# Fewer, wider VectorE operations in the convolution of a mixer kernel, and a GpSimd copy that orders its tokens

## Chip, cores, metric

The kernel runs on one core of one Trainium2 chip. The metric is the device time of one execution in microseconds: before the change 1099.98, the median of three runs (1099.77 to 1100.17). One further execution was profiled.

## What is computed

A block over 2048 tokens of 576 channels: a layer norm, then two branches on the normalised tokens, an S4D convolution over time and an MLP over channels, and a gate.

```python
x  = A_u
xn = layernorm(x)
# branch A: kernel K[d, l] = 2 Re sum_n C[d, n] exp(A[d, n] dt[d] l),  l < 2048, 128 modes n
s  = irfft(rfft(xn, 4096) * rfft(K, 4096))[:2048] + xn * D_skip
# branch B: per token, 576 -> 4608 -> 576
h  = gelu(layernorm(xn) @ w1 + b1)
out = x + s * silu(h @ w2 + b2)
```

## The kernel before, in words

**MLP.** The inner dimension is cut into 12 groups of 384 and the tokens into four blocks of 512, which gives 48 slots. A slot is three tiles of the first layer (`layer1`, L599: 14 matmuls of 512 columns each), GELU on ScalarE (L635), a split of the result into a high part (ScalarE, L638) and a low part (VectorE, L641), and the second layer (`layer2`, L662: 72 matmuls of 288 columns), whose sums VectorE adds to `acc` (L672). Numbers are split in this way so that three products of the faster fp32r format stand for one in fp32; weights are split on the fly (L552 on ScalarE, L549 on VectorE). A prologue `pair` (L582) can do two of the remainder matmuls at the edge of a slot as one step.

**Convolution.** Two parts, both on all five engines.

- *Kernel tables* (`tables`, `kgen`), 36 blocks of 16 channels. VectorE makes phases (L897, L900, L906), ScalarE rounds them and takes cosine and sine (L903 to L916), VectorE makes magnitudes (L922) and weighs the phases with them (`weigh`): 32 late columns go to a tile `U` (L933), 32 reversed early ones to one half of `v` (L935), 32 early ones to the other half (L937, and L939 with a minus sign). Each of these is done once for the cosine plane and once for the sine plane. Then PE multiplies `U` with `v` (L978) and ScalarE copies the block out (L983). The phase tile `w` has two buffers.
- *Transforms* (`chunk`), six chunks of 96 channels. Tokens `xc` and kernel `kt` are split (`in_parts`: high L1058 on ScalarE, low L1062 on VectorE; the tokens are read in another order than they lie in memory, so with a step), transformed (`x1` L1082, `k1` L1113), transposed by VectorE in 32x32 blocks from PSUM (L1090, L1121, two halves of a bank pair apiece), transformed again (`s2` L1143), multiplied: ScalarE copies the kernel's spectrum (L1152), VectorE makes four products per frequency in two operations (L1158) and adds and subtracts them (L1164, L1165). Then come the inverse transforms (L1185, L1211) and stores.

**Order.** The order of all instructions is planned in Python while the program is recorded. A class `Order` keeps a clock for each engine; each `step` has an engine, an assumed duration, the marks that it needs and one that it sets. MLP units are placed on PE one after the other. Between them `advance` places steps of VectorE, ScalarE and GpSimd whose needs are met by the assumed clocks, and `pe_turns` places the convolution's PE steps in the gaps between MLP units. A `kgen` can ride in front of `x1`, `k1`, `s2` or another host (`ride`, `lead`), without a gap of its own. Once recorded, each engine works through its instructions in that order and waits on semaphores; the assumed durations have no further effect. GpSimd also issues DMAs, in its one queue: parameters `par` (L879), stores of the convolution's result (L1220), the loads and stores of the last sums (L701 to L713).

Of the kernel before, what the change touches and what calls it, by code (L numbers as in the profile page):

```python
# [9 lines left out]
F32 = mybir.dt.float32  # L10
F32R = mybir.dt.float32r
# [7 lines left out]
P = 128  # L19
# [20 lines left out]
def dve(n):  # L40
    return 0.075 + 0.00104 * n


def act(n):
    return 0.06 + 0.00098 * n
# [165 lines left out]
def mixer_kernel(ctx, tc, u, log_a_real, a_imag, c_real, c_imag, log_dt, d_skip, w1, b1, w2, b2,  # L211
# [558 lines left out]
    def params():  # L770
# [8 lines left out]
        dt = sb.tile([P, 2, SB, 32], F32, name="U").rearrange("p a b c -> p (a b c)")[:, :D]  # L779
# [108 lines left out]
    def tables(b):  # L888
# [36 lines left out]
        def weigh(k, part):  # L925

            if k == 0 and part == 0:
                T["v"] = sb.tile([P, 2, SB, 64], F32, name="v")
                T["U"] = sb.tile([P, 2, SB, 32], F32, name="U")
                TAB[b] = (T["U"], T["v"])  # L930
            w, v, m = T["w"], T["v"], T["m"]
            if part == 0:
                nc.vector.tensor_mul(T["U"][:, k], w[:, k, :, 33:], m[:, :, 64:])  # L933
            elif part == 1:
                nc.vector.tensor_mul(v[:, k, :, :32], w[:, k, :, 32:0:-1], m[:, :, :32])  # L935
            elif k == 0:
                nc.vector.tensor_mul(v[:, k, :, 32:], w[:, k, :, :32], m[:, :, 32:64])  # L937
            else:
                nc.vector.scalar_tensor_tensor(v[:, k, :, 32:], w[:, k, :, :32], -1.0, m[:, :, 32:64],  # L939
                                               op0=OP.mult, op1=OP.mult)  # L940
# [5 lines left out]
                 step("DVE", dve(SB * NV), f(phase, 0), need=[("wu", b - 2, 1)] if b > 1 else []),  # L946
# [6 lines left out]
                + [step("DVE", dve(n), f(weigh, k, part), need=[("sin", b, k)] + ([("kg", b - 1)] if b else []),  # L953
                        mark=("wu", b, k) if part == 2 else None) for k in range(2) for part in range(3)])
# [10 lines left out]
    def kgen(b):  # L965
# [20 lines left out]
        return [step("PE", KG + 0.2, mm, need=need + [("wu", b, 1)], cv=1, mark=("kg", b)),  # L986
# [23 lines left out]
    def chunk(c):  # L1010
# [41 lines left out]
        def in_parts(which, i, get, m, need):  # L1052

            def high():
                a = sb.tile([P, 2, 4 * CH], F32R, name="pr").rearrange("p t c -> p (t c)")
                b = sb.tile([P, 2, 4 * CH], F32R, name="ys", bufs=2).rearrange("p t c -> p (t c)")
                PARTS2[which, i] = [t.rearrange("p (c b) -> p c b", b=m) for t in (a, b)]
                nc.scalar.activation(PARTS2[which, i][0], get(), AF.Copy)  # L1058

            def low():  # L1060
                a, b = PARTS2[which, i]
                nc.vector.tensor_sub(b, get(), a.bitcast(F32))  # L1062

            n = 768 if which == "k" else 2000
            four.append(step("ACT", act(n), high, need=need))
            four.append(step("DVE", dve(n), low, mark=(which + "p", c, i)))

        def x1(i):
# [18 lines left out]
            for d0 in (0, 24):  # L1087
                for e in range(2):
                    c0 = 48 * i + d0 + 12 * e
                    add("DVE", 0.65, lambda d0=d0, e=e, c0=c0: nc.vector.transpose(  # L1090
                        A2[:, :, 0, c0:c0 + 12].rearrange("p k d r -> p d k r"), Q[d0][:, e]), cv=-e)

        def k1(i):
# [7 lines left out]
            in_parts("k", i, lambda: KT[c, i], 64, [("k1", c, i - 1) if i else ("x1", c, CH // 48 - 1)])  # L1101
# [18 lines left out]
            for g in range(4):  # L1120
                add("DVE", 0.65, lambda g=g: nc.vector.transpose(  # L1121
                    A2[:, :, 1, 48 * i + 12 * g:48 * i + 12 * g + 12].rearrange("p k d r -> p d k r"),
                    Q[g // 2 * 2][:, g % 2]),
                    cv=-(g % 2))

        def s2(p):
# [5 lines left out]
            def mm():  # L1132
# [5 lines left out]
                for i in range(2):  # L1138
                    for ri in range(2):
                        for q in range(4):  # L1140
                            for f in range(2):
                                r = slice(64 * f, 64 * f + 64)
                                nc.tensor.matmul(Q[i][32 * q:32 * q + 32, f, 2 * ri:2 * ri + 2],  # L1143
# [6 lines left out]
            def copy(i):  # L1150
                KK[i] = sb.tile([P, 2, 2, CH], F32, name="kk")
                nc.scalar.activation(KK[i], Q[i][:, :, 1::2], AF.Copy)  # L1152

            def prod(i):

                PR[i] = sb.tile([P, 2, 4 * CH], F32, name="pr").rearrange("p t (a b d) -> p t a b d", a=2, b=2)
                for t in range(2):
                    nc.vector.tensor_mul(PR[i][:, t], bc(Q[i][:, t, 0::2], 2, 2), bc(KK[i][:, t], 1, 2))  # L1158

            def sums(i):  # L1160
                if i == 0:
                    Y.append(ys_tile())
                x, y = PR[i], Y[0]
                nc.vector.tensor_sub(y[:, i, 0], x[:, :, 0, 0], x[:, :, 1, 1])  # L1164
                nc.vector.tensor_add(y[:, i, 1], x[:, :, 0, 1], x[:, :, 1, 0])  # L1165
            for i in range(2):
                two.append(step("ACT", act(4 * CH), lambda i=i: copy(i), need=[("s2", c, p)]))
                two.append(step("DVE", 0.95, lambda i=i: prod(i), cv=-1))
                two.append(step("DVE", 0.63, lambda i=i: sums(i), mark=("sum", c, p) if i else None))
# [540 lines left out]
```

## Time and profile before

| | before |
|---|---|
| median of 3 runs | 1099.98 us |
| span of the profiled execution | 1099.5 us |
| VectorE busy | 920.5 us, 1514 instructions |
| ScalarE busy | 696.6 us, 1040 instructions |
| GpSimd busy | 184.6 us, 254 instructions |

The span runs from the first to the last profiled instruction. In the views, PE is TensorE, PEld its weight loads, DVE VectorE, ACT ScalarE, POOL GpSimd and SP the queue engine; a group's row names the line, engine, operation, output <- inputs, shape and count, then busy us, mean ns of one, and the idle time just ahead of them with what ended it. In a timeline, a row starts with start and length in us.

### The profile page before, as it was taken

The numbers are of one execution on the slowest core, as the hardware profiler recorded it, in microseconds if no ns is written. First come the engines' busy times: TensorE is split into PE (matmuls) and PEld (weight loads), VectorE is DVE, ScalarE is ACT, GpSimd is POOL, SyncE is SP. The second block draws the span as 40 slices with busy tenths as digits, with TensorE's granted clock in tenths as the row PEclk, the third lists the DMA queues.
The fourth block names the chain that finished last, engine by engine and source line by source line (L and its number), as shares of the span: only waits on it lengthen the run. The fifth ranks groups of instructions, "written<-read, shape, count | busy, mean of one in ns | idle before, by whom it ended". The sixth has DMA issues, their size and how long they took to land.

```text
span 1099.5 us, 27206 instructions
## 1 busy us (share of the span) xinstructions
PE 1090.1 (99%) x11447; PEld 953.9 (87%) x11447; DVE 920.5 (84%) x1514; ACT 696.6 (63%) x1040; POOL 184.6 (17%) x254
## 2 busy tenths in 40 slices
PE   9999999999999999999999999999999999999997
PEld 7989899889888888888998888888888888888896
DVE  7798678979998899999999998898998986765356
ACT  6585699866666675676865857566675754325233
POOL 5566211170110100001100000000100012110220
PEclk9999999999999999999999999999999999999999
DMA  8746655734444152455623314242333426453453
GB/s 230 235 144 156 232 162 196 215 75 126 154 124 145 48 112 57 116 121 143 150 57 94 91 56 126 39 147 60 90 92 77 143 65 180 117 177 108 126 149 94
DMA packets 139683, 138.23 MB, mean 126 GB/s; under 512 B 88952, under 2 KB 105016, under 8 KB 138984
## 3 DMA queue, kind: packets, MB, share of 16 engines
q1 hardware_dynamic: 124664, 85.49, 29.5%
q0 software_dynamic: 14336, 50.12, 14.8%
q8 instruction: 89, 1.46, 0.6%
q10 hardware_dynamic: 560, 0.89, 0.3%
q14 instruction: 34, 0.28, 0.1%
HBM read 102.17 MB, written 36.63 MB: 126 GB/s over the span
## 4 chain that ended last, share of the span: by engine, by line
PE 96%; SPq 1%; DMA 1%; DVE 1%; issue 0%; ACT 0%; ACTq 0%; DVEq 0%
PE mxb L662 21%; PE mxa L662 21%; PE mxa L599 20%; PE mxb L599 20%; PE cv L1143 3%; PE cv L978 3%; PE cv L1185 2%; PE cv L1211 2%; PE cv L1113 1%; PE cv L1082 1%; DMA w<-in_A_u_dram 1%; SPq L791 1%; PE mxa L614 0%; SPq L383 0%; DMA acc<-in_A_u_dram 0%
## 5 line engine op out<-in xcount | busy, mean ns | idle before, releaser
L641 DVE TENSOR_TENSOR hl<-h,hh 128x512 fp32r<-128x512 f32 x144 | 99.1, 691 | 88.3 <-ACT hh L638 87.6
L662 PE MATMUL mxb<-w2h,hh 128*128 128x288 f32 x576 | 171.6, 298 | 0.0
L662 PE MATMUL mxa<-w2h,hh 128*128 128x288 f32 x573 | 170.8, 298 | 0.0
L662 PE MATMUL mxb<-w2h,hl 128*128 128x288 f32 x576 | 170.1, 295 | 0.3 <-DVE hl L641 0.3
L662 PE MATMUL mxb<-w2l,hh 128*128 128x288 f32 x576 | 169.5, 294 | 0.0
L662 PE MATMUL mxa<-w2h,hl 128*128 128x288 f32 x573 | 169.1, 295 | 0.0
L662 PE MATMUL mxa<-w2l,hh 128*128 128x288 f32 x573 | 168.6, 294 | 0.0
L635 ACT ACTIVATE h<-mxa,b1t 128x512 f32<-128x512 f32 x73 | 50.2, 688 | 111.8 <-PE mxa L599 110.1
L662 PEld LDWEIGHTS mxa<-w2h,hh 128*128 128x128 f32 x573 | 107.6, 188 | 6.6 <-issue 3.5
L662 PEld LDWEIGHTS mxb<-w2h,hh 128*128 128x128 f32 x576 | 108.1, 188 | 5.7 <-issue 1.5
L662 PEld LDWEIGHTS mxb<-w2l,hh 128*128 128x128 f32 x576 | 108.1, 188 | 0.6
L662 PEld LDWEIGHTS mxb<-w2h,hl 128*128 128x128 f32 x576 | 108.1, 188 | 0.5 <-DVE hl L641 0.5
L662 PEld LDWEIGHTS mxa<-w2l,hh 128*128 128x128 f32 x573 | 107.6, 188 | 0.6
L662 PEld LDWEIGHTS mxa<-w2h,hl 128*128 128x128 f32 x573 | 107.5, 188 | 0.0
L879 POOL DMA_DIRECT2D par<-par_s x36 | 27.8, 773 | 464.2 <-DVE mg L922 459.5
L638 ACT ACTIVATE hh<-h 128x512 fp32r<-128x512 f32 x144 | 90.6, 630 | 3.6
L635 ACT ACTIVATE h<-mxb,b1t 128x512 f32<-128x512 f32 x71 | 48.9, 689 | 68.9 <-PE mxb L599 66.5
L672 DVE TENSOR_TENSOR acc<-mxa,acc 128x576 f32<-128x576 f32 x87 | 65.5, 752 | 31.4 <-PE mxa L662 31.0
L672 DVE TENSOR_TENSOR acc<-mxb,acc 128x576 f32<-128x576 f32 x88 | 66.1, 752 | 16.0 <-PE mxb L662 15.5
L599 PE MATMUL mxa<-XH,w1h 128*128 128x512 f32 x284 | 79.1, 400 | 0.0
L599 PE MATMUL mxb<-XH,w1h 128*128 128x512 f32 x280 | 77.8, 399 | 0.0
L599 PE MATMUL mxa<-XL,w1h 128*128 128x512 f32 x284 | 76.1, 390 | 0.0
(261 smaller groups left out, 2485.9 us busy)
## 6 DMA issues: line engine op xcount, KB each, us to landing
raw<-in_B_w_dram SPq DMA_DIRECT2D x72, 288.0 KB, 3.5
raw<-in_B_w_dram SPq DMA_DIRECT2D x96, 192.0 KB, 3.8
par_s<-A POOLq DMA_DIRECT2D x4, 2160.0 KB, 8.2
par<-par_s POOLq DMA_DIRECT2D x36, 240.0 KB, 3.6
f2t<-f2q SPq DMA_DIRECT2D x24, 256.0 KB, 3.3
g2t<-g2p SPq DMA_DIRECT2D x24, 256.0 KB, 4.0
bias<-XR SPq DMA_DIRECT2D x42, 128.0 KB, 3.8
raw<-in_B_w_dram SPq DMA_DIRECT2D x48, 96.0 KB, 4.0
```

Source lines behind the costliest of these rows:

```text
L599: nc.tensor.matmul(q, a, b, start=j == 0 and i not in BEGUN, stop=j == len(ops) - 1, skip_group_check=True)
L635: nc.scalar.activation(t, q, AF.Gelu_apprx_tanh, bias=b1t[:, k:k + 1], scale=1.0)
L638: LAST[0] = nc.scalar.activation(hh[:, i], t, AF.Copy)
L641: nc.vector.tensor_sub(hl[:, i], t, hh[:, i].bitcast(F32))
L662: nc.tensor.matmul(q[:, dh, :288], a[:, i, c], b[:, i, d], start=i == 0 and k == 0 and not alone, stop=i == G - 1 and k == 2)
L672: nc.vector.tensor_add(o, q[:, dh:dh + n, :288], b)
L791: nc.sync.dma_start(r[32 * g:32 * g + 32].rearrange("c (b n) -> c b n", n=32), dram(src[k], 32 * g, [[N, 32], [32 * N, D // 32], [1, 32]]))
L879: nc.gpsimd.dma_start(PAR[b].rearrange("p (g i) k -> p g (i k)", g=4), dram(par_s, (b // 3 * 48 + b % 3 * 4) * NPAR, [[D * NPAR, P], [12 * ...
L978: nc.tensor.matmul(q[32 * g:32 * g + 32, i // 2, i % 2 * 64:i % 2 * 64 + 64], U[:, ri, 4 * g + i, :], v[:, ri, 4 * g + i, :], start=ri == ...
L1143: nc.tensor.matmul(Q[i][32 * q:32 * q + 32, f, 2 * ri:2 * ri + 2], m[r, 4 * i + q, 32 * ri:32 * ri + 32], A2[r, 4 * p + 2 * i + q // 2, :, ...
L1185: nc.tensor.matmul(QI[q // 2][64 * f:64 * f + 64, q % 2, i], MAT["g2t", p + i // 2][r, i % 2, f, ri], YS[p + i // 2][0][r, i % 2, ri, f], ...
L1211: nc.tensor.matmul(Q[h][64 * y:64 * y + 64, t], g1t.rearrange("p a e -> p (a e)"), A2[:, k:k + 2, 1].rearrange("p i d r -> p i r d"), star ...
```

## The change

- **U over the phases.** The weighed late columns are written over the phase tile's own columns 33 to 64; tile `U` is gone. PE now reads its weights from `w`. The phases of block b so wait for `kgen` of block b-2 (`kg`), no longer for its weighing (`wu`).
- **Weighing.** Where both planes are weighed alike, one operation does both: four operations a block in place of six.
- **Tokens.** GpSimd copies them into the transform's order (`xt`); both split operations read this copy, without a step.
- **Transpositions.** One per bank pair in place of two.
- **Spectra.** `s2` writes the signal's and the kernel's two parts one after the other (`ri::2`), so each matmul's output is two runs of 96 elements in place of one of 192. ScalarE copies the kernel's spectrum with imaginary and real part in exchanged order, and adds a negated copy of the imaginary part. Overlapping views of this copy let one VectorE operation make all four products, and one addition all sums.
- The tile that the parameters' `dt` borrowed is another one, since `U` is gone. Assumed durations and marks of the planner follow.

```diff
-        def weigh(k, part):
-            if k == 0 and part == 0:
+        def weigh(part):
+            if part == 0:
                 T["v"] = sb.tile([P, 2, SB, 64], F32, name="v")
-                T["U"] = sb.tile([P, 2, SB, 32], F32, name="U")
-                TAB[b] = (T["U"], T["v"])
+                TAB[b] = (T["w"][:, :, :, 33:], T["v"])
             w, v, m = T["w"], T["v"], T["m"]
             if part == 0:
-                nc.vector.tensor_mul(T["U"][:, k], w[:, k, :, 33:], m[:, :, 64:])
+                nc.vector.tensor_mul(v[:, 0, :, 32:], w[:, 0, :, :32], m[:, :, 32:64])
             elif part == 1:
-                nc.vector.tensor_mul(v[:, k, :, :32], w[:, k, :, 32:0:-1], m[:, :, :32])
-            elif k == 0:
-                nc.vector.tensor_mul(v[:, k, :, 32:], w[:, k, :, :32], m[:, :, 32:64])
+                nc.vector.tensor_mul(v[:, :, :, :32], w[:, :, :, 32:0:-1], bc(m[:, :, :32], 1, 2))
+            elif part == 2:
+                nc.vector.tensor_mul(w[:, :, :, 33:], w[:, :, :, 33:], bc(m[:, :, 64:], 1, 2))
...
-                 step("DVE", dve(SB * NV), f(phase, 0), need=[("wu", b - 2, 1)] if b > 1 else []),
+                 step("DVE", dve(SB * NV), f(phase, 0), need=[("kg", b - 2)] if b > 1 else []),
...
+            def turn():
+                T["x"] = sb.tile([P, 24, m], F32, name="xt")
+                nc.gpsimd.tensor_copy(T["x"], get())
...
-                nc.scalar.activation(PARTS2[which, i][0], get(), AF.Copy)
+                nc.scalar.activation(T["a"], source(), AF.Copy)
...
-                nc.vector.tensor_sub(b, get(), a.bitcast(F32))
+                nc.vector.tensor_sub(T["b"], source(), T["a"].bitcast(F32))
...
+            if which == "x":
+                four.append(step("POOL", 2.3, turn, need=need))
+            four.append(step("ACT", act(768), high, need=need))
+            four.append(step("DVE", dve(768), low, mark=(which + "p", c, i)))
...
-                for e in range(2):
-                    c0 = 48 * i + d0 + 12 * e
-                    add("DVE", 0.65, lambda d0=d0, e=e, c0=c0: nc.vector.transpose(
-                        A2[:, :, 0, c0:c0 + 12].rearrange("p k d r -> p d k r"), Q[d0][:, e]), cv=-e)
+                c0 = 48 * i + d0
+                add("DVE", 0.9, lambda d0=d0, c0=c0: nc.vector.transpose(
+                    A2[:, :, 0, c0:c0 + 24].rearrange("p k d r -> p d k r"), Q[d0]), cv=-1)
...
-                                nc.tensor.matmul(Q[i][32 * q:32 * q + 32, f, 2 * ri:2 * ri + 2],
+                                nc.tensor.matmul(Q[i][32 * q:32 * q + 32, f, ri::2],
...
-                nc.scalar.activation(KK[i], Q[i][:, :, 1::2], AF.Copy)
+                nc.scalar.activation(KK[i][:, :, :2], Q[i][:, :, :1:-1], AF.Copy)
+                nc.scalar.activation(KK[i][:, :, 2], Q[i][:, :, 3], AF.Copy, scale=-1.0)
...
-                for t in range(2):
-                    nc.vector.tensor_mul(PR[i][:, t], bc(Q[i][:, t, 0::2], 2, 2), bc(KK[i][:, t], 1, 2))
+                nc.vector.tensor_mul(PR[i], bc(x, 2, 2), k)
...
-                nc.vector.tensor_sub(y[:, i, 0], x[:, :, 0, 0], x[:, :, 1, 1])
-                nc.vector.tensor_add(y[:, i, 1], x[:, :, 0, 1], x[:, :, 1, 0])
+                nc.vector.tensor_add(y[:, i].rearrange("p a t d -> p t a d"), x[:, :, :, :CH], x[:, :, :, CH:])
```

More of the change, by code (lines that the diff above doesn't have):

```diff
@@ L952, in tables @@
                  step("DVE", dve(n), f(mags, 1), mark=("mags", b))]
[L953 to L954 removed]
+                + [step("DVE", dve((1, 2, 2, 1)[part] * n), f(weigh, part), need=[("sin", b, part > 0)]
+                        + ([("kg", b - 1)] if b else []), mark=("wu", b) if part == 3 else None) for part in range(4)])
     KT = {}
```

41 lines of the change are left out of this document (20 added, 21 removed).

## The prediction

> **What bounds the kernel now.** I read the page first: engine shares, then the granted clock, then the chain that ended last.
>
> ```profile
> span 1099.5 us, 27206 instructions
> PE 1090.1 (99%) x11447; PEld 953.9 (87%) x11447; DVE 920.5 (84%) x1514; ACT 696.6 (63%) x1040; POOL 184.6 (17%) x254
> PEclk9999999999999999999999999999999999999999
> PE 96%; SPq 1%; DMA 1%; DVE 1%; issue 0%; ACT 0%; ACTq 0%; DVEq 0%
> ```
>
> PE is busy 1090.1 of 1099.5 us, at full clock in every slice, and 96% of the last chain is PE. VectorE is at 84%, but the chain holds 1% of it. A busy PE can still hide waits, since ends of matmuls are modelled, so the waits of PE come next (five rows in all; the two left out belong to the start-up), and one stretch of 200 us from the middle.
>
> ```profile
> PE mxa L1273 <- POOL XL L1266: 1.3, 1, 1.3
> PE cv L1143 <- issue: 0.6, 1, 0.6
> ...
> PE mxb L662 <- DVE hl L641: 0.3, 1, 0.3
> ```
>
> ```profile
> 600.00:800.00 200.00, 199.41 (x2632) 170.65 (x2631) 181.18 (x289) 133.73 (x177) 11.11 (x14) 1.00 0.31 84
> ```
>
> After the start PE waits twice in the whole execution, 0.6 us once (L1143, the second spectrum transform `s2`) and 0.3 us once (L662). The window's columns are length, then busy time of PE, PEld, DVE, ACT, POOL: PE misses 0.59 us of 200 while VectorE works 181. Nothing that VectorE, ScalarE or GpSimd does in this kernel is waited for by PE, except by luck of fractions of a microsecond. The end is the last matmul and a fixed tail:
>
> ```profile
> 1092.84 0.29 PE L662 MATMUL cv<-w2h,hl 128*128 128x288 f32 x1
> ```
>
> It ends at 1093.1, so 6.4 us of last gate, sum and store follow. The change touches none of them.
>
> So the time is the sum of PE's work plus two small waits, and the question for each edit is only: does it change PE's work, or make PE wait?
>
> **The change: PE's own work.** The instruction order of the two built programs shows the same 3456, 1946, 1152, 768, 768, 288, 144 and 48 matmuls of MLP layers and convolution steps, and 14 `pair` prologues in each. What differs is where the convolution's groups stand between the MLP's matmuls: PE leaves the MLP for a group 84 times before and 86 times after (without the start), and the kernel-table groups (`kgen`) that ride in front of another group go from 18 of 36 to 16. What a ride is worth can be read from three places of the timeline: `s2` alone, `kgen` with `s2`, `kgen` alone.
>
> ```profile
> 717.37 0.29 PE L662 MATMUL mxa<-w2h,hl 128*128 128x288 f32 x1
> 717.59 1.59 PE L1143 MATMUL cv<-A,f2t 64*32 64x192 f32 x64
> 719.11 0.40 PE L662 MATMUL mxb<-w2h,hh 128*128 128x288 f32 x1
> 719.34 0.30 PE L662 MATMUL mxb<-w2l,hh 128*128 128x288 f32 x1
> 719.48 0.29 PE L662 MATMUL mxb<-w2h,hl 128*128 128x288 f32 x1
> ```
>
> ```profile
> 744.29 0.29 PE L662 MATMUL mxa<-w2h,hl 128*128 128x288 f32 x1
> 744.51 1.10 PE L978 MATMUL cv<-v,U 128*32 128x64 f32 x64
> 745.54 1.61 PE L1143 MATMUL cv<-A,f2t 64*32 64x192 f32 x64
> 747.08 0.40 PE L662 MATMUL mxb<-w2h,hh 128*128 128x288 f32 x1
> ```
>
> ```profile
> 648.82 0.29 PE L662 MATMUL mxa<-w2h,hl 128*128 128x288 f32 x1
> 649.03 1.10 PE L978 MATMUL cv<-v,U 128*32 128x64 f32 x64
> 650.07 0.40 PE L662 MATMUL mxb<-w2h,hh 128*128 128x288 f32 x1
> ```
>
> An MLP matmul starts every 0.13 to 0.14 us (719.34 to 719.48). From the last one before a group to the first behind it: 1.74 us for `s2`, 2.79 for both, 1.25 for `kgen`. Less one normal step each that is 1.61, 2.66 and 1.12, and the second step after the return is 0.10 too long each time (719.11 to 719.34, against 0.13). A ride therefore saves 1.61 + 1.12 + 0.10 - 2.66 = 0.17 us. Two rides fewer: **+0.3 us**.
>
> The wait at L1143 stood here:
>
> ```profile
> 621.04 1.59 PE L1143 MATMUL cv<-A,f2t 64*32 64x192 f32 x61
> 623.22 0.53 PE L1143 MATMUL cv<-A,f2t 64*32 64x192 f32 x3 [0.59 <-issue]
> ```
>
> The last three of 64 records come late; against the normal 1.6 us the group loses 1.1 us. The trace names no releaser ("issue"), so it isn't VectorE's work that was late. The place is re-ordered by the change, so it may vanish (-1.1) or turn up elsewhere (0). I take the middle, **-0.5**. The 0.3 us at L662 lies ahead of the first transform, where both programs have the same PE order, and stays.
>
> Two PE instructions change form, and no row shows the new forms. `s2` writes each result as two runs of 96 instead of one of 192 (the spectra of signal and kernel are interleaved differently), and `kgen` takes its weights out of the phase table `w`, at a row step of 65 instead of 32. The floor for both is 0: same columns, same contraction, nothing that could shorten them. For the ceiling the trace offers only the groups' whole time: 24 groups of `s2` at 1.6 us are 39 us, 36 of `kgen` at 1.1 us are 40. A slowdown by a tenth would be 4 us for either. I take 0, because a matmul's rows here go by its columns (192 columns in 64 records at 1.6 us, 64 columns in 64 records at 1.1 us), and these don't change.
> The Trainium skill speaks against this edit: its page "PSUM — Partial Sum Buffer", section Specifications (TRN2), says that PSUM has 8-byte cachelines and that any non-contiguous access pattern slows matmuls significantly. No row of this trace has such an output; taken literally it is the third rival below, and with runs of 96 elements I read it as meaning short steps.
>
> **The change: the other engines.** These sums are off the path; they say how much room there is.
>
> ```profile
> L933 DVE TENSOR_TENSOR U<-w,mg 128x512 f32<-128x512 f32 x72 | 49.3, 684 | 3.7 <-PE cv L978 2.3 <-ACT w L914 0.7
> L922 DVE TENSOR_TENSOR mg<-par 128x1024 f32<-128x1024 f32 x36 | 44.0, 1223 | 0.7
> L1158 DVE TENSOR_TENSOR pr<-cv,kk 128x384 f32<-128x384 f32 x96 | 48.7, 550 | 2.0 <-ACT kk L1152 1.8
> L1121 DVE STREAM_TRANSPOSE A<-cv 128x384 f32<-128x384 f32 x48 | 24.5, 556 | 2.7 <-PE cv L1113 2.7
> L1164 DVE TENSOR_TENSOR ys<-pr 128x192 f32<-128x192 f32 x48 | 17.0, 355 | 1.0
> L1062 DVE TENSOR_TENSOR ys<-xc,pr 128x768 fp32r<-128x768 f32 x12 | 24.7, 2057 | 2.0 <-ACT pr L1058 2.0
> L1062 DVE TENSOR_TENSOR ys<-kt,pr 128x768 fp32r<-128x768 f32 x12 | 11.1, 928 | 0.0
> L1058 ACT ACTIVATE pr<-xc 128x768 fp32r<-128x768 f32 x12 | 25.2, 2103 | 13.1 <-DMA xc<-xn_s 12.8 <-DVE w L900 0.3
> L1058 ACT ACTIVATE pr<-kt 128x768 fp32r<-128x768 f32 x12 | 10.1, 838 | 3.8 <-PE cv L1082 3.3 <-ACT w2h L552 0.3 <-PE cv L1113 0.3
> L1152 ACT ACTIVATE kk<-cv 128x384 f32<-128x384 f32 x48 | 23.1, 482 | 24.7 <-PE cv L1143 13.8 <-DVE pr L1158 10.9
> L432 POOL TENSOR_SCALAR w<-w,mv,rs 128x576 f32<-128x576 f32 x6 | 16.5, 2755 | 17.4 <-ACT w2h L552 9.5 <-ACT h L635 7.8
> L549 POOL TENSOR_TENSOR w1l<-raw,w1h 128x384 fp32r<-128x384 f32 x2 | 2.0, 1018 | 0.1
> ```
>
> Weighing, 36 tables: six operations of 512 elements become two of 512 and two of 1024: 36 x (4 x 0.684 - 2 x 1.223) = 10.4 us less. Products: 96 x 0.55 become 48 of 768 elements at about 0.93 (the 768-element subtraction): 8 less. Sums: 96 x 0.355 become 48 of 384 at 0.55: 7.7 less. Transpositions: 96 x 0.556 become 48 at 0.93 to 1.11: 0 to 9 less. Low parts of the tokens: 12 x (2.06 - 0.93) = 13.5 less. VectorE gives up some **45 of 920 us**. ScalarE saves 12 x (2.10 - 0.84) = 15 on the tokens' high parts and adds 48 negated half-size copies, at most 48 x 0.48 = 23 and about half of that: even. GpSimd gains 12 copies of 768 elements. Its nearest rows put one between 2 x 1.02 = 2.0 us (L549, scaled) and 2.75 x 768 / 576 = 3.7 us (L432, scaled); if the strided read costs it the factor 2.10 / 0.84 that it costs ScalarE, 5.1. I take 2.8, between the two rows of its own.
>
> The path to the first transform `x1` was 2.10 + 2.06 = 4.2 us from loaded tokens to both parts; it becomes 2.8 + 0.84 + 0.93 = 4.6 (3.8 to 6.9). ScalarE's high part now waits for GpSimd, and behind it in ScalarE's queue stand GELUs of the next MLP tile, for which VectorE and then PE wait. The cover is shown by a place where that same step waited far longer:
>
> ```profile
> 940.63 2.11 ACT L1058 ACTIVATE pr<-xc 128x768 fp32r<-128x768 f32 x1 [9.94 <-DMA xc<-xn_s]
> 930.06 1.06 POOL L713 DMA_DIRECT2D out_dram<-row  x2 [10.17 <-DVE row L710]
> ```
>
> ScalarE stood 9.9 us for its tokens and the list of PE's waits has no entry for it. If that cover is missing, 12 transforms late by 0.4 us (at most 2.7) cost 5 us (at most 32).
>
> GpSimd's copy also runs beside VectorE. While GpSimd worked on 128x576 from 64.89 to 67.18, a VectorE subtraction took 0.92 us instead of its mean of 0.69 (this row and the mean are from the timeline and page):
>
> ```profile
> 64.89 2.29 POOL L432 TENSOR_SCALAR w<-w,mv,rs 128x576 f32<-128x576 f32 x1
> ```
>
> ```profile
> 65.34 0.92 DVE L641 TENSOR_TENSOR hl<-h,hh 128x512 fp32r<-128x512 f32 x1 [0.56 <-ACT hh L638]
> ```
>
> ```profile
> L641 DVE TENSOR_TENSOR hl<-h,hh 128x512 fp32r<-128x512 f32 x144 | 99.1, 691 | 88.3 <-ACT hh L638 87.6
> ```
>
> Some three VectorE operations beside each copy, 0.23 us each, are 12 x 0.7 = 8 us given back of the 45, also off the path.
> The Trainium skill's "GPSIMD Engine Reference", section Specifications, has GpSimd's SBUF interfaces shared with VectorE when that has two SBUF inputs; the row of 0.92 us agrees.
>
> Holding `w` until `kgen` is done makes the next-but-one phase table wait for PE, on VectorE. Queued behind it are splits that PE needs; with two buffers of `w` the wait is for a table two back, and 36 tables in 1099.5 us come every 30 us on average. I cost it at nothing; if the cover goes, it is rival 1's kind of wait.
>
> **Sum.** 1099.5 + 0.3 - 0.5 = 1099.3 us of span. The runs' median, 1099.98, is 0.5 over the profiled span, so **1099.8 us**, no change.
>
> **Rivals.** (1) *The token copy makes PE wait, slower.* GpSimd takes its queue in order, and in the built order several token copies stand behind its own DMA issues: the second one of the last chunk behind two output stores that wait for a VectorE sum (as the row at 930.06 does, 10.2 us, and 1.06 us for the issue) and three loads. ScalarE's high part waits for the copy, a GELU behind that, then its low part, then PE. It decides from the point where a copy is later than ScalarE's idle time at its place; a third of the 12 places, late by 1 to 3 us, gives 4 to 12: 1104 to 1112. For it: a copy of 2.8 us may be 5.1. Against: 9.9 us were hidden before, and VectorE gets emptier. Chance 0.14. (2) *VectorE was the hidden bound, faster.* Then the 45 us would show up on PE. Against it: PE has 1.1 and 0.3 us to give after the start. Even all of it gives 1099.98 - 1.4 = 1098.6; under 1097.8 only if PE's instructions themselves get shorter. Chance of that 0.03. (3) *The new forms slow PE*, a tenth of `s2` or `kgen` or both: +4 to +8, 1104 to 1108; a doubling of `s2` gives 1139. Chance 0.06. That the edit doesn't do what it says is excluded by the instruction counts (VectorE 1514 to 1298).
>
> **Chances and range.** A run tells 0.2% (2.2 us) from no change. No change: 0.77, with 1098.6 to 1101.5 for it; slower 0.20 (0.14 + 0.06); faster 0.03. The range goes from 1098.5 (both waits gone, no price for rides) to 1104.0, where the two slower rivals begin, and leaves under 0.2 out.
>
> **What would show it.** PE busy near 1090 with the same matmul counts; VectorE near 875 to 885; PE's waits still below 2 us after the start; `s2` alone still 1.6 us and `kgen` 1.1; GpSimd copies at 2 to 3.7 us. It is wrong if PE's waits name VectorE or ScalarE for over 2 us, if `s2`'s 64 records take over 1.7 us, or if PE's busy time itself moves by more than 1 us.

## The result: 1.0% slower, and the profile after

The changed kernel takes **1110.72 us** (median of four runs, 1110.58 to 1111.95), the kernel before 1100.08 in the same comparison (1099.77 to 1100.33): 1.0098 times as long, interval 1.0084 to 1.0112. That is 10.6 us more, outside the range of the prediction, and inside that of its first rival. The profiled execution took 1110.59 us for a span of 1108.8.

The page of the changed kernel, engine shares and the chain that ended last:

```profile
span 1108.8 us, 27048 instructions
PE 1092.7 (99%) x11447; PEld 954.8 (86%) x11447; DVE 908.9 (82%) x1298; ACT 703.4 (63%) x1096; POOL 211.2 (19%) x266
PEclk9999999999999999999999999999999999999999
PE 87%; DVE 8%; ACT 2%; issue 1%; DMA 1%; SPq 1%; DVEq 0%; ACTq 0%
```

PE's busy time has risen by 2.6 us only and its records are the same 11447, but the chain has gone from 96% PE and 1% VectorE to 87% and 8%: PE now waits, and for VectorE. The list of PE's waits names the places (the entries left out are those of the start-up):

```profile
PE mxa L662 <- DVE hl L641: 3.0, 2, 2.2
PE mxb L662 <- DVE acc L672: 2.0, 2, 1.4
...
PE mxb L662 <- DVE hl L641: 0.9, 2, 0.7
PE mxa L662 <- DVE acc L672: 0.7, 1, 0.7
...
PE cv L1191 <- issue: 0.5, 1, 0.5
...
PE mxb L662 <- ACT h L635: 0.2, 1, 0.2
```

Counted from the start of one matmul to the start of the next, less the normal step, these and some shorter gaps are 9.3 us after the start-up, against 1.2 before (the views list fewer, 7.3 and 0.9, since a matmul's modelled end covers the first 0.2 us of a gap); the last matmul ends at 1102.5 instead of 1093.1, and the tail behind it is unchanged at 6.3. So nearly all of the loss lies in some ten stalls of the MLP's second layer, at 222, 389, 486, 530 to 555, 693 and 959 us. The question is what makes VectorE late, with 11.6 us less to do.

The groups of the changed kernel that answer to the prediction's prices:

```profile
L1057 POOL COPY xt<-xc 128x768 f32<-128x768 f32 x12 | 27.9, 2327 | 45.5 <-DVE ys L1069 24.0 <-DVE acc L672 11.0 <-DMA xc<-xn_s 10.6
L1066 ACT ACTIVATE pr<-xt 128x768 fp32r<-128x768 f32 x12 | 10.0, 834 | 3.9 <-POOL xt L1057 3.9
L641 DVE TENSOR_TENSOR hl<-h,hh 128x512 fp32r<-128x512 f32 x144 | 102.7, 717 | 95.8 <-ACT hh L638 95.4
L922 DVE TENSOR_TENSOR mg<-par 128x1024 f32<-128x1024 f32 x36 | 49.9, 1386 | 0.8
L1165 DVE TENSOR_TENSOR pr<-cv,kk 128x768 f32<-128x768 f32 x48 | 45.7, 952 | 4.1 <-ACT kk L1158 4.0
```

The copy is as long as estimated, 2.33 us. But two groups of VectorE that the change doesn't touch have grown in the mean: L641 from 691 to 717 ns, L922 from 1223 to 1386. A mean of 36 that moves by 163 ns hides a few that moved by microseconds. The timeline finds them at the first two stalls (the copy, VectorE's operation beside it, and the matmul that waited; at the second stall also the operation that it waited for):

```profile
220.97 3.38 DVE L641 TENSOR_TENSOR hl<-h,hh 128x512 fp32r<-128x512 f32 x1 [2.48 <-ACT hh L638]
...
221.58 2.21 POOL L1057 COPY xt<-xc 128x768 f32<-128x768 f32 x1
...
224.41 0.40 PE L662 MATMUL mxa<-w2h,hl 128*128 128x288 f32 x1 [2.22 <-DVE hl L641]
```

```profile
384.25 2.08 POOL L1057 COPY xt<-xc 128x768 f32<-128x768 f32 x1 [9.59 <-DVE ys L1069]
...
384.64 2.25 DVE L641 TENSOR_TENSOR hl<-h,hh 128x512 fp32r<-128x512 f32 x1 [0.45 <-ACT hh L638]
...
390.06 0.71 DVE L672 TENSOR_TENSOR acc<-mxb,acc 128x576 f32<-128x576 f32 x1
...
390.82 0.40 PE L662 MATMUL mxb<-w2h,hh 128*128 128x288 f32 x1 [1.38 <-DVE acc L672]
```

L641 normally takes 0.69 us. Here it ends 0.56 us after the copy does, both times (224.35 against 223.79, 386.89 against 386.33): it seems to stand until the copy is through. At the second stall PE doesn't wait for this L641, but for an L672 that comes 3.2 us later: VectorE works without a pause in between, so the lateness is handed on. Of the twelve copies, eight have one such operation beside them, lengthened by 1.6 to 2.7 us, 15.7 us in all; beside the other four VectorE reads from PSUM, at its normal speed.

### The profile page after: what moved, and what is told of

Read it like the earlier page. It is cut to its first block, busy times and chain, and to the rows that moved or that the text cites. A ratio compares the mean times of both kernels' runs of the same rounds, so it can differ in the third digit from the quotient of the medians.

```text
span 1108.8 us, 27048 instructions
## 1 busy us (share of the span) xinstructions
PE 1092.7 (99%) x11447; PEld 954.8 (86%) x11447; DVE 908.9 (82%) x1298; ACT 703.4 (63%) x1096; POOL 211.2 (19%) x266
## 4 chain that ended last, share of the span: by engine, by line
PE 87%; DVE 8%; ACT 2%; issue 1%; DMA 1%; SPq 1%; DVEq 0%; ACTq 0%
PE mxb L662 19%; PE mxa L662 19%; PE mxa L599 18%; PE mxb L599 18%; PE cv L1148 3%; PE cv L977 3%; PE cv L1191 2%; PE cv L1120 1%; PE cv L1217 1%; DVE hl L641 1%; PE cv L1090 1%; DVE mg L922 1%; DVE w L897 1%; DVE acc L672 1%; SPq L452 1%
## 5 line engine op out<-in xcount | busy, mean ns | idle before, releaser
L641 DVE TENSOR_TENSOR hl<-h,hh 128x512 fp32r<-128x512 f32 x144 | 102.7, 717 | 95.8 <-ACT hh L638 95.4
L672 DVE TENSOR_TENSOR acc<-mxa,acc 128x576 f32<-128x576 f32 x87 | 65.3, 751 | 28.7 <-PE mxa L662 28.4
L672 DVE TENSOR_TENSOR acc<-mxb,acc 128x576 f32<-128x576 f32 x88 | 66.1, 751 | 22.4 <-PE mxb L662 21.9
```

The costliest lines, as they stand in the source:

```text
L641: nc.vector.tensor_sub(hl[:, i], t, hh[:, i].bitcast(F32))
L672: nc.vector.tensor_add(o, q[:, dh:dh + n, :288], b)
```

## The experiments

**Theories.** T1: GpSimd's stepped copy keeps VectorE from its SBUF inputs for as long as it reads; what PE needs next stands behind it. T2 (rival): the copy only delays ScalarE, as rival 1 of the prediction has it. T3: wide operations by themselves, or the new order that they lead to, make VectorE late. T4: holding `w` makes the tables and with them the whole convolution late. The recorded expectations number them otherwise: their theory 1 is T1, theory 2 is T3 and theory 3 is T4. All runs beside the kernel before on the same chip; its medians there were 1100.14 (e1 to e4), 1100.94 (e5 to e8), 1100.52 (e9, e10, e11, e14), 1099.87 (e12, e13, e15, e16) and 1100.42 (e17).

### The copy: e1, e4, e7, e8

e1 leaves the copies out and reads the tokens in memory order, so that its transforms work on unordered tokens; PE, VectorE, ScalarE and SP keep their order.

```diff
...
-                nc.gpsimd.tensor_copy(T["x"], get())
+                pass
...
-                return get() if which == "k" else T["x"].rearrange("p c b -> p (c b)")
+                return get() if which == "k" else XC[i].rearrange("p b d -> p (b d)")
```

> The changed kernel with GpSimd's 12 token copies left out and nothing put in their place: the planner still counts 2.3 us of GpSimd for each, so the order on PE, VectorE, ScalarE and the SP queue is the same to the last instruction. ScalarE and VectorE split the tokens in the order in which they lie in memory, so the transform gets its tokens in the wrong order (the result is not the reference's); its operations have the same size. Theory 1 (while GpSimd copies, VectorE's operations with two SBUF inputs stand still, and the lateness reaches PE): the waits at 222, 389, 549 to 555, 693 and 958 us go, 7 to 8 us of the 9; 1102 to 1104 us, and no VectorE subtraction of 512 elements over 1 us in the transforms' time. Theory 2 (wider VectorE operations and the new order by themselves make urgent ones late): 1109 to 1111 us, the waits stay where they are.

1104.11 us, ratio 1.0036 (1.0023 to 1.0048), just over the range of theory 1. The waits at 222, 389, 693 and 958 us go, those up to 555 stay. **The copies cost 6.6 of the 10.6 us**, 4.0 are something else. VectorE's busy time falls from 908.9 to 893.4: the twelve copies had lengthened it by 15.5 us.

e4 copies by a scaling by 1 in place of a plain copy, e7 steps through the write and not the read, e8 copies in four quarters:

```diff
-                nc.gpsimd.tensor_copy(T["x"], get())
+                nc.gpsimd.tensor_scalar(T["x"], get(), 1.0, None, op0=OP.mult)             # e4
+                nc.gpsimd.tensor_copy(T["x"].rearrange("p d b -> p b d"), XC[i])           # e7
+                for n in range(0, 24, 6): nc.gpsimd.tensor_copy(T["x"][:, n:n + 6], get()[:, n:n + 6])   # e8
```

> The changed kernel with GpSimd's copy written as a multiplication by 1.0 (a one-input operation with a constant), same order on every engine. The page of before showed a VectorE subtraction beside GpSimd's 128x576 scaling at 0.92 us, not the 3.4 us that stand beside a copy. Theory 1a (it is the copy's form that shuts VectorE out): 1102 to 1105 us, VectorE's operations beside it under 1.3 us. Theory 1b (any GpSimd operation of that rate shuts it out for its length): 1109 to 1113 us. Theory 2 (wide operations): 1109 to 1111 us with VectorE's rows beside it short.

1113.84, ratio 1.0123, above every range: the same stalls. The scaling lasts 3.4 us and more, yet VectorE's operations beside it are as long as beside the plain copy (L641 3.40 and 2.27 us) and end 0.8 us ahead of the scaling's end; the next ones are normal. VectorE is busy 909.2 us, as in the changed kernel. About 1.7 of the 3.1 us that this run takes longer than the changed kernel lie in a lower granted clock behind the first stall (last section); the rest is not placed.

> The changed kernel with one difference: GpSimd's copy reads the tokens in the order in which they lie and writes them with a step, in place of reading with a step and writing in order. Same order on every engine. In the changed kernel VectorE's two-input operations beside a copy lasted some 1.9 us longer; beside the scaling that replaced it they lasted 1.9 us longer too, although the scaling took 3.4 us. Theory 1c (VectorE is shut out while GpSimd reads with a step): lengthening falls to 0.2 to 0.5 us as beside GpSimd's scaling in the first 100 us of the kernel before, 1104 to 1106 us as without the copies. Rival 1d (any 768 elements through the port shut it out as long): 1110 to 1112 us.

1108.38, ratio 1.0071, between the two ranges: with the step on the write most copies are 1.6 us and the operation beside them is longer by 0.9 to 2.0 us; the stall at 222 goes from 2.4 to 1.65.

> The changed kernel with each token copy cut into four of 192 elements. If VectorE gets in between two GpSimd instructions, no operation is lengthened by more than 0.6 us and 1105 to 1108 us come out; if GpSimd's next instruction takes the port at once, the lengthening stays at 1.9 us or more and the time at 1110 to 1113 us.

1108.64, ratio 1.0071, just over the first range: VectorE gets in between the quarters and loses about 0.45 us per operation, but more operations are hit, and the four pieces together take 3.8 us. The stall at 222 is gone, the one at 389 is not.

VectorE's busy time is 15.8, 10.2 and 13.1 us above that of e1 in e4, e7 and e8: all three lengthen VectorE's operations as T1 has it, and none removes the loss. That VectorE is held for just as long as GpSimd reads, e4 does not bear out.

### The parts alone: e2, e3, e5, e6

e2 is the whole change without the token copy (split operations read with a step, as before); e3 is the kernel before with U over the phases and the copy; e5 has U over the phases alone; e6 has the wide weighings and transpositions alone, with `U` in its own tile.

```diff
 # e5: the kernel before, with
...
-                TAB[b] = (T["U"], T["v"])
+                TAB[b] = (T["w"][:, :, :, 33:], T["v"])
...
-                nc.vector.tensor_mul(T["U"][:, k], w[:, k, :, 33:], m[:, :, 64:])
+                nc.vector.tensor_mul(w[:, k, :, 33:], w[:, k, :, 33:], m[:, :, 64:])
...
-                 ... f(phase, 0), need=[("wu", b - 2, 1)] if b > 1 else []),
+                 ... f(phase, 0), need=[("kg", b - 2)] if b > 1 else []),
```

> The whole change but the token copy: ScalarE and VectorE read the tokens with a step as before, and the planner is told so. Theory 1 (port): PE's waits for VectorE and ScalarE under 2 us, 1098.5 to 1102 us. Theory 2 (wide operations, new order): 1105 to 1110 us. VectorE busy near 1514 to 1298 instructions' worth less: 920 - 34 = about 886 us in both.

1119.98, ratio 1.0185, outside both ranges. PE's waits are few, but the last matmul ends at 1098.0 and the span at 1118.5: the convolution is late, and its end is bare.

> The kernel before with U over the phases (needed for room in SBUF) and the token copy on GpSimd, and the VectorE operations narrow as before. Theory 1 (port): each copy holds up VectorE for 1 to 2.5 us, 5 to 12 us on PE, 1105 to 1112 us. Theory 2 (wide operations): within 2 us of the kernel before, 1098 to 1102 us.

1129.23, ratio 1.0263, outside both ranges: both at once, 14 us of stalls and 18 us of bare tail.

> The kernel before with U over the phases alone: six weighing operations, the phase tile held until the kernel table's matmuls are done. Theory 3 (holding the phases delays the tables and so the whole convolution; what follows the last inverse transform takes some 54 us, as in the two runs that ended 18 to 20 us behind their last matmul, and is bare where that transform starts after about 1045 us): last inverse transform after 1050 us, 1105 to 1125 us, PE's waits under 4 us, the end far behind the last matmul. Rival: U is harmless and those two runs were late for other reasons: 1098 to 1102 us, last inverse transform before 1045 us.

1147.44, ratio 1.0423, above the range of theory 3, by its mechanism: the last inverse transform begins at 1093.0 us. In its trace, the last group of the last inverse transform, and PE around the end (length, PE busy, clock, DMA):

```profile
1095.44 1.57 PE L1210 MATMUL cv<-A,g1t 128*64 128x384 f32 x8 [0.91 <-ACT pr L1218]
```

```profile
1100.00:1145.00 45.00, 0.00 (x0) 0.52 0.63 182
```

The MLP is through and 45 us of stores, loads and last sums follow with nothing on PE to hide them. Before, that transform began at 1024.7, in the whole change at 1047.5, and behind it stand some 53 to 56 us of work (55.7 in e2, 52.7 here). In the whole change 61.3 us are left from there to the end, so it hides them, by this estimate with 6 to 9 us to spare, where the kernel before had 19 to 22. T4 holds for U alone; in the whole change it costs nothing (e17 below, which holds `w` too, loses nothing).

> The kernel before with four weighing operations in place of six (U in its own tile) and one transposition per bank pair; no token copy, spectra as before. Theory 2 (wide VectorE operations by themselves make PE wait): 1103 to 1108 us. Theories 1 and 3 (port, held phases) both expect no loss: 1097 to 1101 us, last inverse transform not later than 1030 us.

1109.45, ratio 1.0077, above the range of theory 2, with a 4.6 us stall at 481 and 1.2 at 492. No copy, no held `w`, and still 8.5 us: this is where the 4.0 us of e1 must be looked for. VectorE stood 6.5 us in front of the transposition of y rows for the MLP's second half (L457), waiting for their DMA, and the accumulation that PE needs stood behind it.

### Why U alone is late: e10

```diff
-                    if b < NB - 1 and od.t["PE"] < h[1] + (ALONE if wait else 3.0):
+                    if b < NB - 1 and od.t["PE"] < h[1] + (1.0 if wait else 1.0):
```

> U alone (1147.44 us; last inverse transform began at 1093 us, 49 us of tail after the last MLP matmul), with the generation of K no longer held back up to 12 or 3 us for a side operation to ride on (1 us in both cases). Theory (w is held until the generation, the generation waits for a ride, and so the next batch's phases start late, table after table): the last generation falls from 1032 us to under 1000, the last inverse transform begins by 1060, and the time is 1100 to 1112, with some 10 single generations more on PE at 0.2 to 0.5 us each. Rival (the delay is in the chain of phases, sines and weighings itself, which now run one table at a time): last inverse transform at 1085 to 1095 and 1140 to 1150 us.

1104.12, ratio 1.0032: 43 us of the 47 come back; the last inverse transform begins at 1035.0. `kgen` waited in the planner for up to 12 us for a group to ride on; harmless while only its own result hung on it, but with `w` held the table after next waits too, and so on through the 36. Its count and times in e5 and here (least, median and longest ns, first and last start):

```profile
L977 PE MATMUL cv<-v,w x2304: 219/219/245, 152.2 to 1032.1; 128*32 128x64 f32 x192
```

```profile
L977 PE MATMUL cv<-v,w x2304: 219/219/245, 153.0 to 949.4; 128*32 128x64 f32 x192
```

### The y rows: e9, e14, e11

First idea: the planner counts 6.5 us from the issue of the loads of a y row to its landing, and VectorE, lighter now, is sent there too early. e9 is e6, e14 the whole change, with 14.0:

```diff
-            ml["steps"].append(step(None, 6.5, load, need=last("t"), mark=M("s", kb)))
+            ml["steps"].append(step(None, 14.0, load, need=last("t"), mark=M("s", kb)))
```

> The run with the wide weighings and transpositions alone (1109.45 us, 4.6 + 1.2 us of PE's waiting at 481 and 492), with one number of the planner changed: it counts 14.0 us instead of 6.5 from the issue of the loads of a y row to the landing. Theory (VectorE, lighter now, is sent to transpose y rows before their DMA has landed, and the w2 accumulations stand behind it): the stall at 481 to 492 goes, 5.8 us less, so 1103 to 1104.5, and VectorE's idle time ahead of L457 falls from 7.6 us to under 1. Rival (wide operations themselves hold VectorE too long at a stretch): the y rows are not what PE waits for in the end, the stall moves to another place, and the time stays at 1108 to 1110.

> The changed kernel with the planner's time from the issue of the y row loads to their landing at 14.0 us instead of 6.5, nothing else. Theory (of the 10.6 us, 6.6 are the copies and 1 to 2 us the y rows that VectorE waits for at 480 to 486): the 0.8 us stall at 486 and part of those at 529 to 555 go, 1108 to 1110. Rival (the copies' stalls only show because VectorE has fallen behind at the y rows): over 4 us less, under 1106.5. Rival (a later plan crowds VectorE later): 1110.5 or more.

1115.11 (ratio 1.013), above both ranges, and 1112.59 (1.0108), in the last rival's: the idea falls. VectorE's wait at L457 is 8.0 and 2.9 us, as long as it was (7.6 and 2.8).

e11 takes T1 at its word and orders the tokens on ScalarE, which before read them with a step anyway:

```diff
-                nc.gpsimd.tensor_copy(T["x"], get())
+                nc.scalar.activation(T["x"], get(), AF.Copy)
-                four.append(step("POOL", 2.3, turn, need=need))
+                four.append(step("ACT", act(2000), turn, need=need))
```

> The changed kernel with the copy that orders the tokens on ScalarE instead of GpSimd (planned there at what ScalarE's stepped read took before, 2.1 us). Theory (the copies cost 6.6 us because GpSimd's copy shuts VectorE's two-input operations out, 1.9 us a time): without GpSimd at work beside them the lengthened rows go (L641 at 222 and 385 us near 0.7 instead of 3.38 and 2.25), and the time is that of the same plan without the copy, 1104, within 1102 to 1106 since the plan moves. Rival 1 (any unit that reads the 768 elements with a step of 24 slows VectorE): the rows stay lengthened and 1109 to 1111. Rival 2 (ScalarE, 12 x 2.1 us heavier, is late with its half of the split or with h): ACT shows as what PE waits for, over 2 us, and the time is 1107 to 1115.

1110.95, ratio 1.0096: in the ranges of both rivals, but without the sign of either. The place at 222 has healed (first row), and an L641 beside ScalarE's copy is not lengthened (the other two):

```profile
221.30 0.69 DVE L641 TENSOR_TENSOR hl<-h,hh 128x512 fp32r<-128x512 f32 x1 [2.48 <-ACT hh L638]
...
553.84 2.09 ACT L1057 ACTIVATE xt<-xc 128x768 f32<-128x768 f32 x1
...
553.96 0.69 DVE L641 TENSOR_TENSOR hl<-h,hh 128x512 fp32r<-128x512 f32 x1 [0.77 <-ACT hh L638]
```

The stalls at 389, 693 and 959 are gone too, and no VectorE operation beside any of the twelve copies is longer than normal: T1 is right in the main, and the step hurts only where GpSimd takes it. T2 falls, since ScalarE copies and splits here one after the other and PE waits for it nowhere after the start-up. What is left is a single stall of 7.2 us at 481.6, and it is the y rows again. SP's queue and VectorE in this run:

```profile
471.46 0.49 SPq L573 DMA_DIRECT2D bias<-XR  x1
477.04 0.32 SPq L1030 DMA_DIRECT2D f2t<-f2q  x1
477.47 1.24 SPq L517 DMA_DIRECT2D raw<-in_B_w_dram  x1
478.76 7.80 SPq L452 DMA_DIRECT2D row<-y_s  x12
```

```profile
476.42 1.02 DVE L549 TENSOR_TENSOR w1l<-raw,w1h 128x384 fp32r<-128x384 f32 x2
483.92 0.71 DVE L457 STREAM_TRANSPOSE row<-row 128x512 f32<-128x512 f32 x1 [6.48 <-DMA row<-y_s]
...
488.29 0.75 DVE L672 TENSOR_TENSOR acc<-mxb,acc 128x576 f32<-128x576 f32 x1
```

The y rows don't land late after their issue (2.9 us in the median); they are issued late. From 472 to 477 SP stands at the load of a table (`f2t`, L1030), which waits for the convolution to free the buffer, and the twelve loads of y rows are behind it in the one queue. VectorE, in its own order, comes to L457 at 477.4 and waits, and with it L672 and PE.

And the stall is dearer than its length. The windows of e11 around it (length, PE busy, granted clock, DMA):

```profile
484.00:485.00 1.00, 0.00 (x0) 1.00 0.40 58
485.00:486.00 1.00, 0.00 (x0) 0.52 0.25 40
...
490.00:492.00 2.00, 2.00 (x10) 0.50 0.88 140
492.00:494.00 2.00, 2.00 (x10) 0.50 0.00 0
...
495.00:496.00 1.00, 1.00 (x8) 0.86 0.00 0
496.00:497.00 1.00, 1.00 (x9) 1.00 0.00 0
```

Some 3.1 us after the last matmul (481.9) the granted clock falls to half, and it stays there for 6.2 us after work has come back at 489.1, with ten matmuls in 2 us in place of fifteen. Work of 6.2 us at half the clock loses 3.1, and that is nearly all that the stall of 7.2 leaves of e11's 10.4 us (the expectations of e12 and e17 put it at 3.7 and 3.8). The Trainium skill's "TensorE: Matmul & The Clock Gate", Part 1, has half the clock after an idle window of about 3.4 us; these rows agree within a few tenths; in e12 below the clock falls only 4.4 us after the last matmul.

### The queue as the cause: e12, e13, e15, e16, e17

e12 (from e11), e13 (from e6), e15 (the kernel before) and e16 (the whole change) issue the table loads from GpSimd; e17 (from e11) leaves these and issues the y rows from GpSimd.

```diff
 # e12, e13, e15, e16
-                nc.sync.dma_start(t, f2q[...
+                nc.gpsimd.dma_start(t, f2q[...
-                nc.sync.dma_start(t, g2p[...
+                nc.gpsimd.dma_start(t, g2p[...
 # e17
-                nc.sync.dma_start(T[0][32 * g:32 * g + 32]...
+                nc.gpsimd.dma_start(T[0][32 * g:32 * g + 32]...
```

> The wide weighings and transpositions alone (1109.45 us; PE waits 4.6 us at 481 and 1.2 us at 492, clock 0.66 from 485 to 490), with the loads of f2t and g2t issued from GpSimd. Theory (SP's queue made the y rows late): both stalls and the low clock go, 1109.45 - 5.8 - 1.7 = 1102, within 1100.3 to 1103. Rival (wide operations by themselves): 1107 or more.

1101.57, ratio 1.0013 (1.0004 to 1.0022): as expected. Both stalls of e6 are gone, VectorE's wait at L457 is 1.2 us. So the wide operations as such cost nothing that can be told (e15, next, is the kernel before with the same table loads and takes 1101.56); T3 is the queue.

> The kernel before with the loads of f2t and g2t issued from GpSimd. In its trace VectorE waited only 0.3 us for y rows and PE not at all there, so no gain is expected: 1100.1, within 1099.5 to 1101. If it is faster by over 0.5 us, part of what e12 and e13 gain is not the change's own loss.

1101.56, ratio 1.0015 (1.0005 to 1.0024): slower by 1.6 us, just outside the range. There is no gain, so what e13 won back is the change's own loss, and against this kernel e13 loses nothing.

> The changed kernel, GpSimd copies and all, with the loads of f2t and g2t issued from GpSimd. Theory (copies 6.6 us, y rows the rest): the 0.8 us at 486 and some of the crowding up to 555 go, 1107 to 1109.5. Rival (table loads and copies on one queue: a copy stands behind a table load that waits for the convolution, and the tokens are late): 1111 or more.

1112.95, ratio 1.0112, in the rival's range. The wait at L457 is 0.0 and the stall at 486 is gone, the copies' stalls remain, and a new one of 2.3 us at 1027 waits for an `f2t` that GpSimd issues late. The granted clock is at half for 3.4 us behind that one and behind the first stall. This settles nothing about the sum.

> The changed kernel with the copy on ScalarE (1110.95 us) and the loads of f2t and g2t issued from GpSimd instead of SP. Theory (the y rows are late because their loads stand in SP's queue behind a table load that waits for the convolution): VectorE's wait at L457 falls from 7.3 us to under 1, the 7.2 us on PE at 481.6 go, the granted clock stays at 1.00 there (normal MLP matmuls 3.8 us shorter in all), so 1110.95 - 7.3 - 3.7 = 1099.9, within 1099 to 1101.5. Rival (the y rows wait for something else, their buffers or y itself): the stall stays, 1108 to 1112. Rival (GpSimd, which now stands at the table loads, is late with the loads of the weighings' parameters): new waits, last inverse transform later than 1060, over 1103.

1114.23, ratio 1.0128: missed. The stall at 481.6 is even 8.3 us, with no table load in SP's queue. SP in this run:

```profile
477.45 0.33 SPq L517 DMA_DIRECT2D raw<-in_B_w_dram  x1
477.83 9.75 SPq L452 DMA_DIRECT2D row<-y_s  x12
```

Its rows before these end at 447.7. Now it is a weight load (L517) that stands until VectorE's splitting (L549, until 477.4) frees its buffer. Which load stands there differs from plan to plan; that the y rows stand behind it does not. So e17:

> The changed kernel with the copy on ScalarE (1110.95 us), the table loads on SP as they were, and the loads of the y rows (L452) issued from GpSimd, which has nothing else between 449.2 and 469.2 us and behind 470 there. Theory (the y rows are late because their loads are queued on SP behind loads that wait for buffers, table loads or weight loads): VectorE's wait at L457 falls from 7.3 us to under 1.5, the wait at 481.6 and the low granted clock behind it (3.8 us of longer matmuls) go: 1110.95 - 7.3 - 3.8 = 1099.9, within 1099 to 1102. Rival (the rows wait for their own buffers or for y): the wait stays over 4 us and the time over 1106.

**1101.50, ratio 1.0007 (0.9998 to 1.0016)**: no difference to the kernel before. VectorE in e17 at the same place:

```profile
476.04 1.02 DVE L549 TENSOR_TENSOR w1l<-raw,w1h 128x384 fp32r<-128x384 f32 x2
476.98 1.30 DVE L457 STREAM_TRANSPOSE row<-row 128x512 f32<-128x512 f32 x2
...
480.44 0.75 DVE L672 TENSOR_TENSOR acc<-mxb,acc 128x576 f32<-128x576 f32 x1
```

The two transpositions start without a wait, PE doesn't wait there, and the clock stays at 1.00 until the MLP is through. With the copy off GpSimd and the y rows off SP's queue, all of the change's loss is gone, and its 28 us of lighter VectorE (892.2 against 920.5) bring nothing, as PE is the bound. (The kernel before with its y rows on GpSimd was not run; VectorE waits 0.3 us for them there.)

**What stays open.** In the changed kernel itself the copies' 6.6 us are shown by leaving them out. Of the other 4.0, e1's trace has 1.1 us at 483 with the y rows, 1.5 at 527 to 555, and about 0.9 more than before at 45 to 47; that the middle ones follow from the first was not tried, some 0.5 us are not placed, and the changed kernel with its copies on GpSimd and only the y rows off SP's queue was not run.

## Why the prediction was wrong, point by point

- **PE's own work: right.** Its side groups take 0.5 us less in all, stalls included, against 0.2 less forecast. PE's busy time rose by 2.6 us all the same, over the 1 us that the prediction took for a sign of being wrong; these are the stalls again, of which the view counts 2 us as busy. `s2` alone is still 1.6 us and `kgen` 1.1 with the new forms, and the third rival falls:

```profile
736.73 1.59 PE L1148 MATMUL cv<-A,f2t 64*32 64x192 f32 x64
751.56 1.10 PE L977 MATMUL cv<-v,w 128*32 128x64 f32 x64
```

  What the Trainium skill's "PSUM — Partial Sum Buffer", section Specifications (TRN2), says of non-contiguous output doesn't show at two runs of 96.
- **The copy's length: right** (2.33 against 2.8, bounds 2.0 and 5.1), and so was the path to `x1`; ScalarE's new wait was 3.9 us over twelve copies, and PE waited 0.2 us for ScalarE. So far the cover of 9.9 us held. Rival 1 had the time (1104 to 1112) by a way that didn't happen, which is luck.
- **Failed: "Some three VectorE operations beside each copy, 0.23 us each ... also off the path."** It is one operation beside eight of the twelve copies and 1.6 to 2.7 us each, 15.5 us in all against 8, and it is on the path where `hl` or `acc` is that operation or stands behind it: 6.6 us (e1). The row it came from, L641 at 0.92 us, stood beside a contiguous scaling; a copy with a step had no row, and the step, weighed for the copy's own length (5.1), was not weighed for its neighbour. The Trainium skill's "SBUF — State Buffer", section "SBUF: two separate sides", has VectorE fully blocked while GpSimd holds the shared ports. Beside a stepped copy the traces agree (ends 0.56 us behind the copy's, twice); beside the contiguous scaling (0.92 us) and the stepped one of e4 (ends 0.8 us ahead of the scaling's) they don't.
- **Failed: "Nothing that VectorE, ScalarE or GpSimd does in this kernel is waited for by PE."** True of the order before, and carried over to another order. There VectorE came to L457 at 477.3, behind y rows issued from 471.8 on; the lighter VectorE comes there with the loads still queued on SP. The re-ordering was weighed for PE's rides alone, not for what stands in SP's queue ahead of what VectorE waits for.
- **Half wrong: holding `w`, "I cost it at nothing".** Nothing in the sum, but not by the cover named: the wait piles up from table to table and comes out at the tail, 47 us by itself; in the whole change the tail has room for it, an estimated 6 to 9 us more than it needs. That it cost nothing there is partly luck.
- **VectorE's gain was mis-sized:** 45 us forecast, 27.1 without the copies (e1). In the trace before, operations in a row start 0.08 us before the last one's end:

```profile
478.56 0.69 DVE L641 TENSOR_TENSOR hl<-h,hh 128x512 fp32r<-128x512 f32 x1 [0.51 <-ACT hh L638]
479.17 0.70 DVE L457 STREAM_TRANSPOSE row<-row 128x512 f32<-128x512 f32 x1
479.79 1.92 DVE L549 TENSOR_TENSOR w1l<-raw,w1h 128x384 fp32r<-128x384 f32 x4
```

  216 operations fewer at 0.08 us are 17 us that were counted and never spent: 45 - 17 = 28. This is worked out, not tried by a run.
- **The offset was mis-sized too:** time and span of one execution differ by some 1.8 us in the profiled executions (1110.59 against 1108.8), not by 0.5; by that the profiled one of before was itself some 1.2 us above the median. Small beside the rest.

## What to carry to other kernels

When PE is the bound and waits nowhere, lightening another engine can gain nothing, and where its order is planned it may lose: each change of a cost re-orders all queues, so ask of every load that the relieved engine will want earlier what stands ahead of it in its queue. Moving work to GpSimd is not free for VectorE: where a copy reads with a step, price VectorE's next operation with two SBUF inputs by the copy's whole length, and move it to ScalarE where that has room. A tile that saves an operation by being held longer makes its buffer's next user wait for the last reader; see what that reader waits for.

## What the runs showed of the hardware

- A GpSimd copy of 128x768 fp32 that reads with a step of 24 elements (2.1 to 3.1 us) keeps a VectorE operation with two SBUF inputs until its end: 0.69 us became 2.25 and 3.38, L922's 1.22 up to 3.58. Operations with an input from PSUM beside a copy stayed normal (L672 0.72 to 0.76, the transpositions 0.94 to 0.97). A contiguous scaling of 2.3 us added at most 0.33 to the subtractions beside it (L641 0.23), and a scaling with a step (3.4 us) as much as the copy. Spans on GpSimd are rough in this profile.
- The clock fell after a shorter idle time too, and late. In e9 PE stood 2.27 us up to 898.30, ran at full clock for 1.5 us, and then at half for 3.4:

```profile
898.00:899.00 1.00, 0.70 (x5) 1.00 0.73 214
899.00:900.00 1.00, 1.00 (x9) 0.89 0.82 190
900.00:901.00 1.00, 1.00 (x6) 0.50 0.90 206
...
903.00:904.00 1.00, 1.00 (x8) 0.90 0.00 0
```

  The length of the idle time doesn't decide it alone. The first stall of the changed kernel (2.22 us up to 224.4) stands at the same place, 2.22 to 2.25 us long, in e4, e14 and e16. In the changed kernel's trace the clock stays up behind it; in the other three it is at half for 3.4 us, which loses 1.7. The same window in the changed kernel and in e4:

```profile
226.00:229.00 3.00, 3.00 (x25) 1.00 1.16 216
```

```profile
226.00:229.00 3.00, 3.00 (x15) 0.50 0.99 139
```

  What decides was not tried. It fits that e16's one run with a mean clock of 0.999 took 1109.26 us and its three at 0.996 to 0.997 took 1112.14 to 1114.03.
